# K and V of a head in three pieces (48, 32, 48 KB per partition) in place of four of 32 KB, in a ring lapped twice per head

## Chip, cores, metric

One core of a Trainium2 chip. The metric is the device time of one execution in microseconds (us), lower is better. The kernel has one stream of DMA transfers, issued by SyncE (its queue is "SPq" in the profile); TensorE (PE), VectorE (DVE) and ScalarE (ACT) work behind it.

## The reference, cut

One decode step of a transformer layer: layer norm, q projection, attention of 32 query heads over 8 K/V heads with 65536 keys each, output projection, residual, layer norm, gated feed-forward. K and V in bf16 are 16 MiB each per head, so nearly all of the 282 MB read is cache.

```python
q = (x @ wq).reshape(B, Sq, Hq, Dh) ...                 # Hq = 32, Hkv = 8, Dh = 128, Sk = 65536
scores = jnp.einsum("bhqd,bhkd->bhqk", q, k) * (Dh ** -0.5)
p = _softmax(scores, axis=-1)
o = jnp.einsum("bhqk,bhkd->bhqd", p, v)
return o...reshape(B, Sq, Hq * Dh) @ wo
# then h = x + that; h2 = h + (sigmoid(n(h) @ w_gate) * (n(h) @ w_up)) @ w_down
```

## The kernel before

A **chunk** is 4 KB per partition (16 keys of 128 elements). A block of K or V is 8 chunks, 32 KB per partition, 4 MiB in all; a head has four of each. The ring in SBUF has four such slots. The order of loads is K of a block, then V of the block one head earlier, and each load waits until the block that had its slot is done: a K block is done when DVE has transposed its chunks (mark `F`), a V block when PE has multiplied it (`PV`).

```python
order = [("wq", 0)]
order += [("K", b) for b in range(NR)]                      # NR = 4 blocks per head
for b in range(NR, NB):                                     # NB = 32 blocks in all
    order += [("K", b), ("V", b - NR)]
order += [("V", NB - 4), ("V", NB - 3), ("V", NB - 2), ("V", NB - 1), ("wg", 0), ("wu", 0), ("wd", 0)]
# ... slot_of[ld] = i % NSLOT, prev[ld] = order[i - NSLOT]   (NSLOT = 4; the last ones are placed by hand)

def freed(ld):
    ...
    return {"wq": "q", "K": f"F{b}", "V": f"PV{b}"}[k]
# ... each load: deps = [freed(prev[ld])]; wo (into the transposed K's space) waits for G7, the last maxima
```

DVE transposes each chunk into one of 8 work buffers, and after the eighth sets the mark, without waiting for anybody:

```python
def dve_block(b):
    s = slot_of[("K", b)]
    for c in range(NC):                                     # NC = 8 chunks
        ...
        op("dve", lambda e, d=dst, sr=src: e.transpose(d, sr), deps, f"T{b}.{c}", to="T")
    op("dve", lambda e: e.memset(scr[:, b:b + 1], 0.0), (), f"F{b}")
    # after a head's last block: maxima of the scores, then mark G
```

PE works per head in four parts: the scores of K block r of this head, then the products of V block r of the head before. Part 3 begins with the maxima of the scores and the softmax, so its products come last of all. A block's products are four rounds of 8 matmuls in a loop in registers; `p` and `v` are the addresses in the weights and in the ring.

```python
goto("sums", "values")
pv_regs(e)                                                  # 14 addresses from p and v
goto("products", "sums")
section("B")                                                # 8 matmuls
e.reg_alu(p, p, 2 * 512, ALU.add)
e.reg_alu(v, v, 2 * 2 * CH, ALU.add)
e.reg_alu(m, m, -1, ALU.add)
e.br_ne(m, 0, on_true="sums", on_false="sums_end")
```

Of the kernel before, what the change touches and what calls it, by code (L numbers as in the profile page):

```python
# [213 lines left out]
def bass_sequential_preLN__gqa_block_cached__glu_gated_glu__decode_kernel(  # L214
# [10 lines left out]
    SLOT = T * DH  # L225
    CH = TC * DH
    NF = FF // 128
# [6 lines left out]
    with ExitStack() as es:  # L234
# [16 lines left out]
        ring = sb("ring", [128, NSLOT * SLOT], bf16)  # L251
# [50 lines left out]
        def slot_ap(s):  # L302
            return ring[:, s * SLOT:(s + 1) * SLOT]

# [4 lines left out]
        order = [("wq", 0)]  # L309
        order += [("K", b) for b in range(NR)]  # L310
        for b in range(NR, NB):
            order += [("K", b), ("V", b - NR)]
        order += [("V", NB - 4), ("V", NB - 3), ("V", NB - 2), ("V", NB - 1), ("wg", 0), ("wu", 0), ("wd", 0)]
        slot_of, prev = {}, {}
        for i, ld in enumerate(order):
            if ld[0] == "V" and ld[1] >= NB - NR:
                slot_of[ld] = slot_of["V", ld[1] - 2]
                prev[ld] = ("V", ld[1] - 2)
            elif ld[0][0] == "w" and i:
                slot_of[ld] = 3 if ld[0] == "wd" else 1  # L320
                prev[ld] = ("K", NB - 1 if ld[0] == "wd" else NB - 2)
            else:
                slot_of[ld] = i % NSLOT
                prev[ld] = order[i - NSLOT] if i >= NSLOT else None

        def freed(ld):
            if ld is None:
                return None
            k, b = ld
            return {"wq": "q", "K": f"F{b}", "V": f"PV{b}"}[k]  # L330

        dma("act", lambda e: e.dma_start(x_col[:, :], A_x[0].rearrange("o (p k) -> (o p) k", k=4)), "x", name="x")
        V_SPLIT = [(0, 3), (3, 4)]
        W_SPLIT = {"wg": [(0, 4)], "wu": [(0, 3), (3, 4)]}
        W_AT = {"wg": 0, "wu": 4 * FF}
        for ld in order:
            k, b = ld
            s = slot_of[ld]
            dst = slot_ap(s)
            deps = [freed(prev[ld])]  # L340
            if k == "wq":
                dma("sp", lambda e, d=dst: e.dma_start(d.rearrange("p (k n) -> p k n", k=4),
                    A_wq.rearrange("(p k) n -> p k n", p=128)), f"r{s}", deps, "wq")
            elif k in ("wg", "wu"):
                w = B_w_gate if k == "wg" else B_w_up
                dst, src = dst[:, W_AT[k]:W_AT[k] + 4 * FF], w.rearrange("(p k) n -> p (k n)", p=128)
                for i, (k0, k1) in enumerate(W_SPLIT[k]):
                    dma("sp", lambda e, d=dst, w=src, a=k0 * FF, z=k1 * FF: e.dma_start(d[:, a:z], w[:, a:z]),
                        f"{k}{i}", deps if i == 0 else (), f"{k}.{i}")
            elif k == "wd":  # L350
                src = B_w_down.rearrange("(p r) n -> p r n", p=128)
                for i, (r0, r1) in enumerate(WD_SPLIT):
                    dma("sp", lambda e, d2=dst[:, r0 * D:r1 * D].rearrange("p (r n) -> p r n", n=D), sr=src[:, r0:r1, :]:
                        e.dma_start(d2, sr), f"wd{i}", deps if i == 0 else (), f"wd{i}")
            else:
                h, r = b // NR, b % NR
                cache = A_k_cache if k == "K" else A_v_cache
                src = cache[0, h, r * BLK:(r + 1) * BLK, :].rearrange("(p t) d -> p (t d)", t=T)
                if ld == ("V", NB - 1):
                    for i, (c0, c1) in enumerate(V_SPLIT):  # L360
                        d2, s2 = (ap[:, 2 * c0 * CH:2 * c1 * CH] for ap in (dst, src))
                        dma("sp", lambda e, d2=d2, s2=s2: e.dma_start(d2, s2),
                            "v0" if i else "vl", deps if i == 0 else (), f"V{b}.{i}")
                else:
                    dma("sp", lambda e, d=dst, sr=src: e.dma_start(d, sr), f"v{s}" if k == "V" else f"k{s}" if k == "K" and b >= NR else f"r{s}",
                        deps, f"{k}{b}")
            if ld == ("V", NB - 4):
                for i, (j0, nj) in enumerate(WO):
                    src = A_wo[j0 * DH:(j0 + nj) * DH, :].rearrange("(p r) n -> p (r n)", r=nj)
                    dst = ktw[:, j0 * D:(j0 + nj) * D]  # L370
                    dma("sp", lambda e, src=src, dst=dst: e.dma_start(dst, src), f"wo{i}",
                        [f"G{HKV - 1}"] if i == 0 else (), f"wo{i}")
# [81 lines left out]
        def project_q(e):  # L454

            e.reg_mov(reg(e, 0), addr_of(xz, 8 + 7))
            e.reg_mov(reg(e, 4), addr_of(ring, slot_of[("wq", 0)] * SLOT))
# [3 lines left out]
            with e.Fori(0, HKV):  # L461
                for kt in range(4):
                    mm_at(e, ps(1, 0, 512, 0, 8), at_reg(xz, reg(e, kt), [[4 * 16, 128], [1, 8]]),
                          at_reg(ring, reg(e, 4 + kt), [[NSLOT * SLOT, 128], [1, 512]]), False, 32)
                for kt in range(4):
                    e.reg_alu(reg(e, kt), reg(e, kt), 2, ALU.subtract)
                for kt in range(4):
                    e.reg_alu(reg(e, 4 + kt), reg(e, 4 + kt), 1024, ALU.add)
# [32 lines left out]
        def dve_block(b):  # L501
            s = slot_of[("K", b)]
            for c in range(NC):
                n = b * NC + c
                at = s * SLOT + (2 * (c % NR) + c // NR) * CH
                src = ring[:, at:at + CH].bitcast(fp32)
                dst = ktw[:, (n % NKT) * CH:(n % NKT + 1) * CH].bitcast(fp32)
                deps = [f"K{b}"] if c == 0 else []
                if b % NR or b == 0:
                    deps.append(f"S{b - 1}.{c}" if b else None)  # L510
                op("dve", lambda e, d=dst, sr=src: e.transpose(d, sr), deps, f"T{b}.{c}", to="T")  # L511
            op("dve", lambda e: e.memset(scr[:, b:b + 1], 0.0), (), f"F{b}")
# [62 lines left out]
        def pv_regs(e):  # L575
            for half in range(NC // NR):
                for tq in range(4):
                    i = 8 * half + tq
                    if i:
                        e.reg_alu(reg(e, i), R["p"], 2 * (128 * tq + half), ALU.add)  # L580
                        e.reg_alu(reg(e, i + 4), R["v"], 2 * (half * TC + 4 * tq) * 128, ALU.add)

        def pv(b):
            h, r = b // NR, b % NR
            if r == NR - 1:
                P.part["pe"] = ("VL", b)
                op("pe", lambda e: None, [f"V{b}" if b < NB - 1 else f"V{b}.1"])
            P.part["pe"] = ("B", b)
            for half in range(NC // NR):
                for tq in range(4):  # L590
                    i = half * 8 + tq
# [3 lines left out]
                        at_reg(ring, reg(e, i + 4) if i else R["v"], [[NSLOT * SLOT, 128], [1, 512]]), False, 32, 32 * tq),  # L595
                       (), f"PV{b}" if half and tq == 3 else None, times=NR)

        def head_out(h):
            op("act", lambda e: e.activation(po_sb[:, :], ps(PO, 0, 512), AF.Copy, scale=rl[:, :]),  # L599
               [f"PV{NR * h + NR - 1}", f"rl{h}"], f"po{h}", to="po")  # L600
# [68 lines left out]
        def pe_flow(e, section):  # L669
# [7 lines left out]
            i, w, p, v, m, k = (R.setdefault(n, e.alloc_register(f"r_{n}")) for n in "iwpvmk")  # L677
            w0, p0 = addr_of(ktw, W0 + NC - 1 + 127), addr_of(PT_sb, 31 * 4)
            v_even, v_odd = (addr_of(ring, slot_of[("V", b)] * SLOT) for b in (0, 1))
            e.reg_mov(i, 0)  # L680
            goto("head")
            e.reg_mov(w, w0)
            e.reg_mov(p, p0)
            goto("part")
# [13 lines left out]
            e.reg_mov(m, NR)  # L698
            e.reg_mov(k, 0)
            e.reg_mov(v, v_even)  # L700

            def odd_late():
                e.reg_mov(v, v_odd)
                e.reg_mov(m, NR - 1)
                e.reg_mov(k, 1)
                away("br_eq", i, HKV, "last_values", lambda: section("VZ"), "sums")
                section("V3")

            def odd():
                e.reg_mov(v, v_odd)  # L710
                section("V1")

            away("br_eq", w, w0, "values0", lambda: section("V0"), "sums")
            away("br_eq", w, w0 - 4, "values1", odd, "sums")
            away("br_eq", w, w0 - 12, "values3", odd_late, "sums")
# [5 lines left out]
            e.reg_alu(p, p, 2 * 512, ALU.add)  # L721
# [5 lines left out]
            def rest():  # L727
                pv_regs(e)
                e.reg_mov(m, 1)
# [7 lines left out]
            e.reg_alu(p, p, 4 - 2 * NR * 512, ALU.add)  # L737
# [7 lines left out]
            away("br_eq", w, w0 - 4, "rows_of_o", lambda: section("L"))  # L745
# [7 lines left out]
        def dve_flow(e, section):  # L753
            with e.Fori(1, HKV):
                for p in ("A0", "B0", "A1", "A2", "A3", "A4"):
# [4 lines left out]
                       "po": ("pe", {"V0": 1, "O": 1}), "v0": ("pe", {"V1": 16, "VL": 16}), "v2": ("pe", {"V0": 16, "V2": 16}),  # L760
                       "Q": ("dve", {"A4": NR * NC + 3}), "D": ("dve", {"A4": 6}), "E": ("dve", {"A4": 4}), "k1": ("dve", {"A4": 32}),
# [110 lines left out]
```

## Time and profile before

| | before |
|---|---|
| time, three runs | 658.1 us median (658.04 to 658.2) |
| span of the profiled run | 657.1 us |
| last landing of the DMA stream | 654.83 us |
| each of the 63 K and V loads of 4 MiB, landing to landing | 9.69 us, within 0.07 |

"Landing" is the moment at which the last of a transfer's 16 completions (one per DMA engine) is recorded in the trace.

In the median a block lands 26 to 29 us after its issue, because others are ahead of it. wq finds an empty queue at time zero and takes 12.3 us for what moves in 9.69: **2.6 us more**.

### The profile page before, as it was taken

How to read it: one execution, taken by the hardware profiler on the slowest of the kernel's cores; microseconds unless marked ns; L12 is line 12 of the kernel's file. 1: busy time of each engine (PE TensorE's matmuls, PEld its weight loads, DVE VectorE, ACT ScalarE, POOL GpSimd, SP SyncE). 2: the span in 40 equal slices, each digit the busy share in tenths (PEclk: the TensorE clock that was granted, in tenths of full speed). 3: DMA queues.
4: the chain of work that ended last, by engine and by line, in shares of the span. 5: the costliest groups of instructions: out<-in, count | busy, mean ns of one | idle time of the engine just before them, and what ended most of it. 6: DMA issues, size and time to landing. Idle time of an engine off the chain costs nothing. (4 is left out here: it accounts for less than half of the span.)

```text
span 657.1 us, 6111 instructions
## 1 busy us (share of the span) xinstructions
PE 420.5 (64%) x2315; PEld 74.1 (11%) x1547; DVE 349.7 (53%) x439; ACT 42.9 (7%) x114; POOL 3.6 (1%) x17
## 2 busy tenths in 40 slices
PE   0688488548666585576765575764866668556746
PEld 0200011011000010010100110101100001001322
DVE  2399775547537665347555374465743575542202
ACT  1100200020000200020000200002000100002001
POOL 1000000000000000000000000000000000000000
PEclk9989689677888697776966769765888869677676
DMA  9999999999999999999999999999999999999998
GB/s 383 447 433 429 439 423 431 431 447 415 447 415 447 437 425 447 415 447 419 443 441 421 447 415 447 423 439 443 419 447 415 447 427 435 445 417 427 435 430 352
DMA packets 10802, 282.34 MB, mean 430 GB/s; under 512 B 1329, under 2 KB 1330, under 8 KB 1842
## 3 DMA queue, kind: packets, MB, share of 16 engines
q1 hardware_dynamic: 10658, 282.33, 99.7%
q10 hardware_dynamic: 144, 0.00, 0.0%
HBM read 282.33 MB, written 0.00 MB: 430 GB/s over the span
## 5 line engine op out<-in xcount | busy, mean ns | idle before, releaser
L431 PE MATMUL PS<-ktw 128*128 128x512 bf16 x1024 | 299.9, 442 | 157.4 <-DVE ktw L511 153.6
L511 DVE STREAM_TRANSPOSE ktw<-ring 128x1024 f32<-128x1024 f32 x256 | 291.6, 1205 | 128.0 <-DMA ring<-in_A_k_cache_dram 128.0
L431 PE MATMUL PS<-ring,PT_sb 128*32 x1024 | 83.9, 455 | 23.6 <-issue 13.2
L431 PEld LDWEIGHTS PS<-ktw 128*128 x256 | 27.1, 106 | 408.2 <-issue 256.8
L565 DVE STREAM_TRANSPOSE PT_sb<-P_sb 128x512 bf16<-128x512 bf16 x32 | 20.2, 684 | 54.0 <-PE PS L602 52.3
L551 ACT ACTIVATE negmax<-PS 128x1 f32<-128x1 f32 x8 | 1.4, 171 | 520.6 <-PE PS L549 520.6
L431 PEld LDWEIGHTS PS<-ring,PT_sb 128*32 x1024 | 25.8, 116 | 79.8 <-issue 74.6
L516 DVE TENSOR_REDUCE M_sb<-PS 128x1 f32<-128x512 f32 x32 | 19.9, 684 | 25.5 <-PE PS L431 25.5
L555 ACT ACTIVATE P_sb<-PS,negmax 128x512 bf16<-128x512 f32 x32 | 21.6, 686 | 0.3
L572 DVE TENSOR_REDUCE lsum<-PS 128x1 f32<-128x4 f32 x8 | 1.3, 163 | 31.2 <-PE PS L570 31.2
L542 PE MATMUL PS<-identf,gm 128*1 128x128 f32 x16 | 3.4, 301 | 16.9 <-DVE gm L540 16.9
L616 DVE TENSOR_TENSOR Lw<-O,blk_of 128x896 bf16<-128x896 bf16 (+1 forms) x2 | 1.4, 683 | 20.6 <-ACT O L606 20.6
L402 PE MATMUL PS<-st,onesf 128*128 128x2 f32 x4 | 1.2, 362 | 16.1 <-DVE st L401 16.1
L431 PE MATMUL PS<-ring,xz 128*8 x32 | 9.2, 459 | 2.3 <-issue 2.3
L599 ACT ACTIVATE po_sb<-PS,rl 128x512 bf16<-128x512 f32 x8 | 5.5, 687 | 53.2 <-PE PS L431 53.2
L431 PE MATMUL PS<-ktw,O 128*1 x26 | 7.6, 464 | 0.0
L549 PE MATMUL PS<-one_f,gmrep 1*128 1x1 f32 x16 | 4.2, 330 | 5.0 <-DVE gmrep L546 5.0
L555 ACT ACTIVATION_READ_ACCUMULATOR P_sb<-PS,negmax 128x1 f32 x32 | 6.5, 202 | 0.0
L476 DVE STREAM_TRANSPOSE qt<-qh 32x512 bf16<-32x512 bf16 x1 | 0.7, 699 | 10.6 <-ACT qh L473 10.6
L602 PE MATMUL PS<-sel_bf,po_sb 128*128 128x4 bf16 x32 | 2.0, 168 | 6.4 <-ACT po_sb L599 6.4
L417 DVE CAST hT<-x_col 128x4 f32<-128x4 bf16 x1 | 0.2, 171 | 10.6 <-DMA x_col<-in_A_x_dram 10.6
L661 DVE COPY yr<-PS 1x512 f32<-1x512 f32 x1 | 0.7, 679 | 8.3 <-PE PS L659 8.3
(82 smaller groups left out, 74.0 us busy)
## 6 DMA issues: line engine op xcount, KB each, us to landing
ring<-in_A_k_cache_dram SPq DMA_DIRECT2D x32, 4096.0 KB, 28.7
ring<-in_A_v_cache_dram SPq DMA_DIRECT2D x31, 4096.0 KB, 26.4
ring<-in_A_wq_dram SPq DMA_DIRECT2D x1, 4096.0 KB, 12.3
ktw<-in_A_wo_dram SPq DMA_DIRECT2D x1, 3584.0 KB, 12.7
ring<-in_A_v_cache_dram SPq DMA_DIRECT2D x1, 3072.0 KB, 13.2
ring<-in_B_w_gate_dram SPq DMA_DIRECT2D x1, 1792.0 KB, 19.0
ring<-in_B_w_up_dram SPq DMA_DIRECT2D x1, 1344.0 KB, 21.7
ring<-in_A_v_cache_dram SPq DMA_DIRECT2D x1, 1024.0 KB, 15.2
```

The source lines that it names most:

```text
L431: return e.add_instruction(mybir.InstMatmult(name=nc.get_next_instruction_name(), engine=mybir.EngineType.PE, ins=[rhs, lhsT], outs=[e.low ...
L511: op("dve", lambda e, d=dst, sr=src: e.transpose(d, sr), deps, f"T{b}.{c}", to="T")
L516: op("dve", lambda e, u=u: e.tensor_reduce(M_sb[:, u % 4:u % 4 + 1], ps(u % NS, 0, 512), AX.X, ALU.max), [f"S{b}.{NC - NR + k}"], f"mx{u}" ...
L542: op("pe", lambda e: e.matmul(ps(MISC, 0, 128, 0, 1), lhsT=gm[:, :], rhs=identf[:, :], start=True, stop=True), [f"gm{h}"], f"gmT{h}", to="Q")
L549: op("pe", lambda e: e.matmul(ps(MISC, 128, 129), lhsT=gmrep[0:1, :], rhs=one_f[0:1, 0:1], start=True, stop=True), [f"gmrep{h}"], f"neg{h}")
L551: op("act", lambda e: e.activation(negmax[:, k:k + 1], ps(MISC, 128, 129), AF.Copy, scale=-att_scale), [f"neg{h}"], f"negmax{h}")
L555: op("act", lambda e, b=b: e.activation(P_sb[:, (b % 4) * 512:(b % 4 + 1) * 512], ps(b % NS, 0, 512), AF.Exp, bias=negmax[:, k:k + 1], sca ...
L565: op("dve", lambda e, b=b: e.transpose(PT_sb[:, (b % 4) * 512:(b % 4 + 1) * 512], P_sb[:, (b % 4) * 512:(b % 4 + 1) * 512]), [f"E{b}", f"o ...
L572: op("dve", lambda e: e.tensor_reduce(lsum[:, :], ps(MISC, 132, 136), AX.X, ALU.add), [f"l{h}"], f"ls{h}", to="D")
L599: op("act", lambda e: e.activation(po_sb[:, :], ps(PO, 0, 512), AF.Copy, scale=rl[:, :]), [f"PV{NR * h + NR - 1}", f"rl{h}"], f"po{h}", to ...
L602: op("pe", lambda e, t=t: e.matmul(ps(OX, 0, 4), lhsT=po_sb[:, t * 128:(t + 1) * 128], rhs=sel_bf[:, 8 * t:8 * t + 8:2], start=(t == 0), s ...
L616: op("dve", lambda e: e.tensor_tensor(Lw[i][:, :].rearrange("p (j c) -> p j c", j=n), bass.AP(tensor=O2, offset=j0, ap=[[NQ, 128], [1, n], ...
```

## The change

The intent is fewer and longer transfers: 48 pieces in place of 64 blocks. As 48 + 32 + 48 KB do not fit fixed slots, the ring's 32 chunks are laid out by hand: K.0 in chunks 0 to 11, V.0 in 12 to 23, K.1 in 24 to 31, V.1 in 0 to 7, K.2 in 8 to 19, V.2 in 20 to 31. A head thus laps the ring twice.

```diff
+    PIECES = ((0, 12), (12, 20), (20, 32))
+    RING = 32 * CH
+    AT = {"K": (0, 24, 8), "V": (12, 0, 20), "K0": (0, 12, 20), "wq": 24, "wg": 12, "wd": 8}
 ...  (loads: the old order, slot_of and freed are gone)
+        for h in range(1, HKV + 1):
+            old = h - 2
+            before_k = (["F0.1"], ["G0"], [f"F{h}.1"]) if h == 1 else ([f"PV{old}.2"], [f"PV{old}.3"], [f"F{h}.1"])
+            before_v = (["F0.3"] if h == 1 else [f"PV{old}.3"], [f"F{h}.0"], [f"F{h}.2"])
+            if h < HKV:
+                for q in range(3):
+                    load("K", h, q, before_k[q], ("ka", "kb", "ka")[q], f"K{h}.{q}")
+                    load("V", h - 1, q, before_v[q], ("va", "vb", "va")[q], f"V{h - 1}.{q}")
+                continue
+            load("V", h - 1, 0, before_v[0], "va", f"V{h - 1}.0")
+            for i, (j0, nj) in enumerate(WO):
 ...              (wo, waits for G7)
+            load("V", h - 1, 1, (), "vb", f"V{h - 1}.1")
 ...              (V.2 in two parts behind PV7.1, then w_gate, w_up, w_down)
 ...  (DVE: the marks that free K's space)
-            op("dve", lambda e: e.memset(scr[:, b:b + 1], 0.0), (), f"F{b}")
+                mark = {7: 0, 11: 1, 19: 2}.get(j, 3 if b == 2 and c == 7 else None)
+                if mark is not None:
+                    op("dve", lambda e, m=4 * h + mark: e.memset(scr[:, m:m + 1], 0.0),
+                       [f"S{b}.{c}"] if mark in (1, 2) else (), f"F{h}.{mark}")
 ...  (PE: the products of a head in parts of 4, 2, 4 and 6 rounds)
+        PARTS = (4, 2, 4, 6)
+            step = (2 * 2 * 512, 2 - 2 * 2 * 512)
             section("B")
-            e.reg_alu(p, p, 2 * 512, ALU.add)
+            e.reg_alu(p, p, s, ALU.add)
+            e.reg_alu(s, s, step[0] ^ step[1], ALU.bitwise_xor)
             e.reg_alu(v, v, 2 * 2 * CH, ALU.add)
```

The mark after chunk j of a head waits for that chunk's scores (`S`) when it is mark 1 or 2. `PV{h}.r` is the end of part r of the products.

## The prediction

> **What bounds the kernel now.** I read the page first, for what is full:
>
> ```profile
> span 657.1 us, 6111 instructions
> PE 420.5 (64%) x2315; PEld 74.1 (11%) x1547; DVE 349.7 (53%) x439; ACT 42.9 (7%) x114; POOL 3.6 (1%) x17
> ...
> DMA  9999999999999999999999999999999999999998
> ...
> PE 1%; DVE 0%; issue 0%; ACT 0%
> ```
>
> The DMA engines are full from the first slice to the last; no compute engine is above 64%; the chain that ended last holds about 1% of the span in compute. So the kernel is one uninterrupted stream of 282.34 MB, plus about 1 us before its first byte (in the windows, 0 GB/s up to 1.0 us) and about 2.5 us after its last (bytes stop between 654 and 655 us). The windows view over two heads' worth of quiet middle gives the rate:
>
> ```profile
> 254.60:293.40 38.80, 23.38 (x112) 3.35 (x68) 21.40 (x26) 2.63 (x8) 0.00 (x0) 0.72 1.00 432
> ```
>
> 432 GB/s, so a 4 MiB block (32 KB per partition) takes 9.70 us, which the timeline repeats: two K starts two blocks apart are at 254.63 and 274.03.
>
> Then the waits of the DMA queue, because a stream can only stay full if the next transfer is issued in time:
>
> ```profile
> SPq L365 <- DVE scr L512: 324.2, 30, 19.4
> SPq L365 <- PE PS L431: 222.4, 29, 18.8
> ```
>
> The issuing queue waits nearly all the time, for a K slot to be transposed (DVE) or a V slot to be multiplied (PE). None of this costs anything today: a transfer lands 26 to 29 us (median) after its issue while it moves for 9.7 us, so over one and a half blocks are queued ahead. That reserve is what the change alters. Last I read the timeline at the end of the last head, the chain from a K landing to the release of V's space:
>
> ```profile
> 583.83 9.13 DVE L511 STREAM_TRANSPOSE ktw<-ring 128x1024 f32<-128x1024 f32 x8 [10.27 <-DMA ring<-in_A_k_cache_dram]
> ...
> 588.51 8.49 PE L431 MATMUL PS<-ktw 128*128 128x512 bf16 x29 [0.54 <-DVE ktw L511]
> ...
> 596.39 2.48 DVE L516 TENSOR_REDUCE M_sb<-PS 128x1 f32<-128x512 f32 x4 [3.42 <-PE PS L431]
> ...
> 598.92 0.80 SPq L371 DMA_DIRECT2D ktw<-in_A_wo_dram  x2
> ...
> 602.45 2.76 PE L431 MATMUL PS<-ring,PT_sb 128*32 x24 [1.75 <-issue]
> ...
> 605.50 1.02 PE L431 MATMUL PS<-ring,PT_sb 128*32 x8 [0.29 <-PEq L169]
> 606.57 8.66 SPq L365 DMA_DIRECT2D ring<-in_A_v_cache_dram  x2
> ```
>
> A head's last K lands at 583.8, is transposed by 592.9, scored by 597.0, its maxima taken, and the last quarter of the previous head's products ends at 606.5; the next V is issued at 606.57. That is 22.7 us from landing to release. The same interval at the other heads (K block landing to the V issue after the head's last products) is 21.4 to 23.4 us. Before the change it is hidden: another V block and then wo are already queued behind.
>
> **What the Trainium skill says.** "DMA: Bandwidth & Descriptors", section "Where 436 GB/s comes from": the ceiling of the 16 ports is 435.2 GB/s. The trace runs at 432, so at most 0.7% is left. Same page, "Why small descriptors are slow": a fixed overhead of about 3 cycles per packet, plus descriptor metadata. The trace agrees in size: 9.70 us per block against 9.64 at 435.2 GB/s. Same page, "Anatomy of one DMA": the DMA engines wait on no semaphore; the issuing sequencer does, before dispatch. The queue's waits above show just that, so one late release holds back everything behind it. "Perfetto Trace Analysis", "DMA Optimizations": larger transfers saturate HBM better, but its example is under 2 KB; at 32 KB this trace has nothing such to gain.
>
> **The change part by part.**
>
> (1) Fewer, longer transfers: 64 blocks of K and V become 48 pieces, and the runs per partition 48, 32 and 48 KB. The whole overhead of the 64 blocks is 64 x (9.70 - 9.64) = about 4 us; a quarter of it goes: **-1 us**. Bytes are the same. A 48 KB piece is an estimated 14.55 us, a 32 KB one 9.70.
>
> (2) The steady head. The ring is still 128 KB, now 32 chunks of 4 KB. Order and places: K.0 in chunks 0-11, V.0 12-23, K.1 24-31, V.1 0-7, K.2 8-19, V.2 20-31. The next head's V.0 overlaps V.2 and waits for part 3 of the products, which reads all of V.2 and comes after all scores and the maxima; the next K.0 waits for part 2. Take the landing of K.2 as zero. V.2 lands at 14.55; K.0 of the next head, if on time, ends at 28.8 (29.1 less 0.3 from last byte to signal). Part 2: four transposes of 1.14 (4.6), the rest of that block's scores (about 13 matmuls of 0.27, to 8.2), four rounds of products (2.2 warm): release near 10.5, first byte 1.0 to 1.2 later, ahead of 14.3. On time, by 2 to 3 us. Part 3: the 22.7 us chain of before (mean of the heads 22.5), plus four more transposes since the piece has 12 chunks (4 x 1.14 = 4.6), plus about 1.5 since PE must do that half block and part 2 first and starts the last scores later, plus two more rounds of products (six for four, 0.6 to 0.7 each after the saved extra wait: 1.3). Release at about 29.9, first byte at 31.1, but the queue is empty at 28.8. **About 2.4 us of idle DMA per head; with PE at its lower clock up to 4.5, with everything warm about 1.** It happens for the V.0 of heads 1 to 6: six times, **+15 us**.
>
> (3) The last head. There is no next K.0 to cover V.0 of head 7, and wo stands behind that V.0 in the queue. So when V.2 of head 6 has landed nothing is queued. The last byte is at 14.3, release at 29.9, first byte at 31.1: **+17 us** in one piece. Before, V and wo filled this hole.
>
> (4) The start. The marks that free K space now wait for scores (after chunks 11 and 19), and DVE stands at them. In the first head DVE is the pace (its row in the timeline is unbroken from 29.0 to 65.2, 1.13 per transpose), so each mark costs the 16 matmuls it waits for, 3.8 us plus hand-over: about 7.8 for both. The head's end mark moves from 70.1 to 78. In before, the next K block's mark came 14.8 later (84.96), so the release for V.1 of head 0 comes near 92.8, first byte at 94; the stream would be empty when K.1 of head 1 is in, which by bytes is 9 blocks and wq from the start, about 89.6. That is 4.4 late. The K.2 behind it waits for scores that are late as well: 1 to 2 more. **+6 us.** If x, on its own small queue, arrives a packet later, add 1.
>
> (5) The end. The last V piece is 32 and 16 KB for 24 and 8; two rounds after the final landing for one (0.8 us), but PE no longer lags behind as it did, and the weights behind are as many bytes as before. **About 0.** The extra register instruction per round is inside the 0.76 us round.
>
> Sum: 658.1 - 1 + 15 + 17 + 6 + 0.5 = **about 696 us**, 5.7% slower.
>
> **The rivals.** (A) *The pieces only remove overhead*: all releases come in time, 657 us. For it: the DMA row is full, compute stands at two thirds. Against it: the average says nothing about a release that is serial after a landing; at least the hole in (3) follows from program order alone. It would need V.0 of head 7 to be released before V.2 of head 6 has landed, which cannot be. (B) *Only the ends lose*: PE is in better clock with longer bursts (the windows show 0.5 to 0.6 of full clock around the maxima), the steady release comes 2 to 3 us earlier, and (2) vanishes: 658 - 1 + 16 + 5 = 678. Speaks for it: the margin is only 2.4 us out of 30. Against: the chain is mostly fixed waits, and part 3 always begins after a pause of PE. (C) *The steady wait is larger*: PE falls to its lower clock for the whole of part 3 (0.92 a round, six rounds) and the late scores (0.3 a matmul), 4.5 to 5 us a head, and the start costs 9: 658 - 1 + 29 + 18 + 9 = 713. (D) *48 KB runs move slower*, from another row pitch in HBM or a split of the runs. Nothing in the trace speaks for it: runs of 32, 28 and 24 KB go at one rate. One per cent of rate would be 6.5 us.
>
> **Range and chances.** The certain part is (3), 15 to 19. (2) spans 6 to 29, (4) 3 to 9. The ends of all together are 681 and 715; 8 in 10 is 682 to 712. The 2% line is 671.3: to stay under it (2) and (4) must both nearly vanish. Slower 0.94, within 2% 0.05, faster 0.01.
>
> **What would show it.** In the profile after: a DMA row with a single low slice near 93 to 95% of the span, some 17 us in which the windows show no bytes, ended by a V issue released by PE; six shorter holes of 2 to 3 us, about 80 us apart, each just before the V.0 that follows a K.0; holes totalling 5 to 8 us between 85 and 110 us; mean near 406 GB/s; the rate between holes 432 to 433, which checks (1). The reading is wrong if the DMA row stays at nines, or if the idle time is there but in front of K.0 (then part 2 is the late release), or if the rate between holes is lower (rival D).

## More of the kernel before

The page's list of DMA issues (last column: median us from issue to landing) shows both:

```profile
ring<-in_A_k_cache_dram SPq DMA_DIRECT2D x32, 4096.0 KB, 28.7
ring<-in_A_v_cache_dram SPq DMA_DIRECT2D x31, 4096.0 KB, 26.4
ring<-in_A_wq_dram SPq DMA_DIRECT2D x1, 4096.0 KB, 12.3
```

The **lead** of a transfer is the landing of the transfer ahead of it minus its own issue: how much time the queue still had in hand when it was issued. Its **loss** is landing, minus the landing ahead, minus its bytes at 9.69 us per 4 MiB. In the kernel before the smallest lead is 4.2 us and only the very first transfer, wq, loses anything.

## The result

| | before | after |
|---|---|---|
| time, six runs each, side by side | 658.24 us (658.04 to 658.39) | 719.02 us (716.85 to 720.74) |
| ratio | | 1.0922 (95%: 1.0904 to 1.0940) |
| span of the profiled run | 657.1 us | 715.5 us |
| last landing | 654.83 us | 713.33 us |

A ratio here is the mean time of one kernel's fast runs over that of the other's fast runs of the same rounds, so not quite the ratio of the medians quoted. The output is correct. The time was predicted as 696 us with a range up to 712: the direction was right, the size 23 us short. The kernel before spent 2.3 us after its last landing, the kernel after 2.2, so the whole 58 us of the two profiled runs lie in the stream.

From the page of the kernel after, first the counts and rows by slice (40 slices of 17.9 us; "DMA" in tenths busy), then the chain that ended last, then one group of instructions, then two kinds of DMA issue:

```profile
span 715.5 us, 6263 instructions
...
DMA  9999989979999799979999899988999899926998
GB/s 410 419 431 393 426 310 396 423 324 427 438 440 426 327 432 438 426 313 433 434 434 393 346 415 450 429 371 355 432 434 420 332 430 437 429 129 280 423 430 348
...
DMA 7%; PE 2%; issue 1%; SPq 0%; DVE 0%; PEldq 0%
...
L498 DVE MEMSET scr<- 1x1 f32 x25 | 1.5, 59 | 66.0 <-PE PS L414 66.0
...
ring<-in_A_k_cache_dram SPq DMA_DIRECT2D x16, 6144.0 KB, 20.4
ring<-in_A_v_cache_dram SPq DMA_DIRECT2D x15, 6144.0 KB, 17.6
```

The nines have dips: one about every 4.6 slices, which is once per head, and one of 2 at the end (129 GB/s). DVE stands 66 us at its marks. The last row is the plainest: half of the 48 KB V pieces land within 17.6 us of their issue, for a transfer that moves in 14.5. They find a dry or nearly dry queue, as wq did.

One head of the kernel after, from the timeline (start, length, engine, line, what, count, in brackets the idle time before it and its releaser):

```profile
287.62 13.64 DVE L495 STREAM_TRANSPOSE ktw<-ring 128x1024 f32<-128x1024 f32 x12 [9.86 <-DMA ring<-in_A_k_cache_dram]
...
298.44 0.63 PE L414 MATMUL PS<-ring,PT_sb 128*32 x8 [0.39 <-issue]
...
299.12 0.33 SPq L322 DMA_DIRECT2D ring<-in_A_k_cache_dram  x1
...
300.08 7.10 PE L414 MATMUL PS<-ktw 128*128 128x512 bf16 x32 [1.00 <-issue]
...
306.56 2.49 DVE L503 TENSOR_REDUCE M_sb<-PS 128x1 f32<-128x512 f32 x4 [5.31 <-PE PS L414]
...
312.60 6.05 PE L414 MATMUL PS<-ring,PT_sb 128*32 x48 [1.93 <-PEq L169]
...
318.69 0.33 SPq L322 DMA_DIRECT2D ring<-in_A_v_cache_dram  x1
```

K.2 lands at 287.59. Part 2 of the products ends at 299.1 and the next K.0 is issued; V.2 lands at 302.09, K.0 at 317.63. Only after the last scores, the maxima and six rounds of products is V.0 issued, at 318.69: 31.1 us after K.2 landed and 1.06 us after the queue ran dry. It lands at 336.30, 17.6 us later. The windows view of the kernel after around that point and before the last head's V.0 (window, length, busy time and count of PE, PEld, DVE, ACT, POOL, granted clock, DMA share, GB/s; a packet is counted in the window in which it starts):

```profile
315.00:317.30 2.30, 2.30 (x24) 0.32 (x16) 0.00 (x0) 0.00 (x0) 0.00 (x0) 0.50 0.06 21
317.40:319.60 2.20, 1.41 (x16) 0.32 (x12) 0.00 (x0) 0.69 (x1) 0.00 (x0) 0.69 0.00 0
632.40:650.00 17.60, 11.42 (x82) 2.07 (x62) 3.14 (x8) 3.65 (x10) 0.00 (x0) 0.90 0.00 0
```

In the first window one packet starts, on one engine of 16 (0.06); in the second none. In the third, 17.6 us long, none either: the hole that the prediction's third term is about. No such window exists in the kernel before.

**The accounts.** Landing by landing, the kernel after loses:

| where | losses (lead in brackets) | sum | predicted |
|---|---|---|---|
| start: V0.0, V0.1, K1.2 | 2.80 (0.45), 3.64 (-1.19), 2.99 (-0.09) | 9.4 | 6 |
| K.0 of heads 2 to 7 | 1.0 to 2.55 (1.6 to 3.0) | 11.2 | 0 |
| V.0 of heads 1 to 6 | 2.3 to 4.1 (-1.06 to 0.32) | 18.9 | 15 |
| V.0 of head 7 | 19.34 (-16.45) | 19.3 | 17 |
| the 14 pieces of 48 KB with over 5 us of lead | -0.036 each | -0.5 | -1 |

Sum 58.5 before rounding; the last landing is 58.5 us later. No other transfer loses more than 0.1, but for wq with 2.6 in both kernels, which is not in the sum. The pieces as such do what they were to do: a 6 MiB piece in an uninterrupted stream lands every 14.50 us, against 14.535 for one and a half old blocks. Everything lost is lost at transfers that were **issued late**.

The two steady rows are one effect, not two. The queue is back at one point in each head: V.0. From K.2's landing to the next one, a head lasts

31.1 (release of V.0) + 17.4 (V.0, issue to landing) + 9.69 (K.1) + 9.69 (V.1) + 14.54 (K.2) = **82.4 us**,

and the mean of the six steady heads is 82.46, against 77.5 without losses. So a loss of K.0 costs nothing of its own as long as V.0's release comes behind it. The prediction's numbers in the same sum: 29.9 + 16.05 + 33.9 = 79.9. It missed 1.2 in the release and 1.4 in V.0's issue to landing, six times: 15 of the 23 us. Its third term missed the same 1.2 and 1.4 once more (19.3 for 17), its fourth 3.4; the rest is that the median run is 2.2 us slower than the profiled one, which was the fastest of six.

**Why an issue 0 to 4 us ahead still costs.** The trace has the 16 completions of each transfer (the 1st, 8th, 15th and 16th in order of completion, us), here for one steady block of the kernel before and four consecutive pieces after; the first line of each is a reference:

```
before  K block       254.34  254.47  254.57  254.61
        next V block  264.02  264.17  264.30  264.35
after   V.2           300.93  301.27  302.03  302.09
        K.0, lead  3.0  315.50  315.86  316.52  317.63     nominal: V.2 + 14.54
        V.0, lead -1.1  335.00  335.48  336.12  336.30
        K.1, lead 17.2  344.68  345.15  345.76  345.95     V.0 + 9.69
```

K.0's first 15 engines are on time to within 0.1 us; **one engine is 1.0 us late, and the transfer has landed only when it has**. At other heads it is two or more of them (head 5: 399.49, 399.77, 401.36, 401.76). In the kernel before the 16 completions of a load lie within 0.25 to 0.44 us of each other; after a late issue they lie 0.7 to 2.4 us apart, and the pieces behind it keep the spread (1.27 to 1.34 us in the four behind the V.0 above). The packet records show where this begins: V.0's first packets start 0.95 us after its issue, and take 2.0 to 3.5 us (mean of the 16: 2.6) where nearly all later ones take 1.82. 0.95, the slowest engine's 1.7, and the usual few tenths from last byte to landing make about the 2.9 us that a dry queue costs a 48 KB piece on average. What makes the first packets slow, the traces do not tell.

The same records account for the uneven loss at small positive leads. K.0 above starts on each engine within 0.01 us of V.2's end there, yet its first packets take 1.81 to 2.52 us, and the one of 2.52 is the last to start. In this run and in experiments 4 and 6 together, 28 transfers have leads of 0.6 to 5 us; in 24 of them the latest end of a first packet is late by the loss itself, to within 0.4 us. (The records do not name the engine; packets were matched to transfers by their order in time.) So the loss depends on where a slow first packet falls: one K.0 of experiment 6 (issued at 442.86, lead 3.5) has first packets of up to 2.81 us and loses 0.03, as they fall on engines with time in hand.

### The profile page after: what moved, and what is told of

It reads as the page before. It is cut to its first block, busy times and chain, and to the rows that moved or that the text cites. A ratio compares the mean times of both kernels' runs of the same rounds, so it can differ in the third digit from the quotient of the medians.

```text
span 715.5 us, 6263 instructions
## 1 busy us (share of the span) xinstructions
PE 426.9 (60%) x2315; PEld 67.7 (9%) x1547; DVE 350.6 (49%) x432; ACT 43.0 (6%) x114; POOL 3.6 (1%) x17
## 5 line engine op out<-in xcount | busy, mean ns | idle before, releaser
L414 PE MATMUL PS<-ktw 128*128 128x512 bf16 x1024 | 294.7, 438 | 173.8 <-DVE ktw L495 159.1
L414 PE MATMUL PS<-ring,PT_sb 128*32 x1024 | 94.6, 474 | 58.0 <-PEq L169 40.0
L414 PEld LDWEIGHTS PS<-ring,PT_sb 128*32 x1024 | 21.2, 116 | 133.3 <-issue 130.4
L498 DVE MEMSET scr<- 1x1 f32 x25 | 1.5, 59 | 66.0 <-PE PS L414 66.0
## 6 DMA issues: line engine op xcount, KB each, us to landing
ring<-in_A_v_cache_dram SPq DMA_DIRECT2D x15, 6144.0 KB, 17.6
ring<-in_A_wq_dram SPq DMA_DIRECT2D x1, 4096.0 KB, 12.3
```

Of the source, the lines that this page charges most:

```text
L414: return e.add_instruction(mybir.InstMatmult(name=nc.get_next_instruction_name(), engine=mybir.EngineType.PE, ins=[rhs, lhsT], outs=[e.low ...
L498: op("dve", lambda e, m=4 * h + mark: e.memset(scr[:, m:m + 1], 0.0), [f"S{b}.{c}"] if mark in (1, 2) else (), f"F{h}.{mark}")
```

## The experiments

The theory: (T1) all of the loss is late issue; the release of V.0 sets each head's period, V.0 of head 7 the end, DVE's waiting marks the start; and a late issue costs more than its lateness. The rivals: (T2) 48 KB runs or the ring's new layout are slower in themselves; (T3) only lateness beyond the queue's end costs, and the rest is something else, such as the added register instructions per round. All kernels below are correct, and each was timed against the kernel before of the same rounds (658.2 to 658.8 us).

### 1. wo ahead of the last head's V.0

```diff
-            load("V", h - 1, 0, before_v[0], "va", f"V{h - 1}.0")
             for i, (j0, nj) in enumerate(WO):
                 ...
+            load("V", h - 1, 0, before_v[0], "va", f"V{h - 1}.0")
```

> The changed kernel, but with wo issued ahead of V.0 of the last head instead of behind it. Theory A (the loss is a late release, and an issue that finds the queue empty costs about 2.9 us plus the time it is late): wo waits for the last head's maxima, which in the changed kernel ended 21.4 us after K.2 landed; V.2 lands 14.5 after it. So wo loses 6.9 + 2.9 = 9.8 us, V.0 then finds wo still moving (issued about 3 us before wo has landed) and loses 0 to 2. Together 10 to 12 us where the changed kernel lost 19.3: 710 to 712 us. Rival B (the hole at the end is not on the path that sets the end, because PE has to finish the last products anyway): no gain, 719.

Measured: **719.6 us** (716.57 to 721.03), ratio 1.0907. The hole became smaller: wo loses 11.0 at a lead of -8.4, V7.0 1.6, and V7.2, now without wo ahead of it, 2.9, together 15.5 in place of 19.3. The time did not follow. The page's chain and the timeline of this run:

```profile
PE 5%; DMA 3%; issue 1%; DVE 1%; ACT 0%; PEldq 0%
```

```profile
643.73 0.80 SPq L340 DMA_DIRECT2D ktw<-in_A_wo_dram  x2
...
652.86 29.32 SPq L322 DMA_DIRECT2D ring<-in_A_v_cache_dram  x4
...
683.15 8.29 PE L414 MATMUL PS<-ktw,O 128*1 x26
...
705.23 1.60 PE L414 MATMUL PS<-ring,PT_sb 128*32 x16 [0.51 <-issue]
```

V7.0 now lands at 672.2, 5.6 us later than in the kernel after (2.7 of these were lost before the last head, whose K.2 lands at 620.8 for 618.2; 3.0 come from the new order), and behind it lies serial work of PE: two parts of products, the rows of the output projection (683 to 691), two more parts. The chain is PE's, and the span ends 7.6 us after the last landing in place of 2.2. Theory A's 710 to 712 missed that, and the number came out as the expectation's rival B had it, but not its reason: in the kernel after the hole was on the path that sets the end (2.2 us from the last landing to the end). Once it was shortened, the gain was **given back on another path**. What follows: the last head's hole is a matter of order, but which transfer fills it has to be chosen with PE's tail in view.

### 2. Marks that do not wait in the first head

```diff
-                       [f"S{b}.{c}"] if mark in (1, 2) else (), f"F{h}.{mark}")
+                       [f"S{b}.{c}"] if h and mark in (1, 2) else (), f"F{h}.{mark}")
```

> The changed kernel, but in the first head the marks after chunks 11 and 19 no longer wait for scores (there are no V reads to protect yet, so this is free of races). Theory A: DVE stands 3.1 and 3.7 us less, the releases of V.0 and V.1 of head 0 and K.2 of head 1 come about 7 us earlier, and the 9.4 us that these three pieces lost (2.8, 3.6 and 3.0) shrink to 0 to 3: 710 to 713 us. Rival B (PE sets the pace of the first head, the marks only stand where DVE would have waited anyway): 718 to 719.

Measured: **714.84 us** (714.68 to 715.87), ratio 1.0855, about 4.2 us less than the kernel after. First the kernel after, then this one, DVE and the first V issue from the timelines:

```profile
47.59 1.24 DVE L495 STREAM_TRANSPOSE ktw<-ring 128x1024 f32<-128x1024 f32 x1 [3.08 <-issue]
...
60.44 1.24 DVE L495 STREAM_TRANSPOSE ktw<-ring 128x1024 f32<-128x1024 f32 x1 [3.72 <-issue]
...
65.11 0.33 SPq L322 DMA_DIRECT2D ring<-in_A_v_cache_dram  x1
```

```profile
45.12 9.12 DVE L495 STREAM_TRANSPOSE ktw<-ring 128x1024 f32<-128x1024 f32 x8
...
57.68 0.33 SPq L322 DMA_DIRECT2D ring<-in_A_v_cache_dram  x1
```

DVE's two pauses of 3.1 and 3.7 us are gone and the releases come 7 to 8 us earlier. The losses at the start fall from 9.4 to 3.3 us, and head 1's K.2 lands 6.0 earlier; about 4 of those are lost again further on (six periods of 82.88 for 82.46, last hole 20.7 for 19.3), so that the two profiled spans differ by 2.0 only. Losses of that size lie within the kernel's own spread (its repeat in experiment 7 has a period of 82.66 and a hole of 20.6). So the marks are the cause of the start's loss.

### 3. A ring of 36 chunks, so that V.0 need not wait for V.2

```diff
-    RING = 32 * CH
+    RING = 36 * CH
-    AT = {"K": (0, 24, 8), "V": (12, 0, 20), ...
+    AT = {"K": (0, 24, 8), "V": (12, 0, 24), ...
-            before_v = (["F0.3"] if h == 1 else [f"PV{old}.3"], ...
+            before_v = (["F0.3"] if h == 1 else [f"G{h - 1}"], ...
```

V.2 moves to chunks 24 to 35 and no longer overlaps V.0, which then waits for the maxima (`G`) alone; V.2 gets a semaphore of its own.

> The changed kernel on a ring of 36 chunks instead of 32: V.2 lies in chunks 24 to 35, no longer over the place of the next V.0, which then waits for the end of its head's maxima (21.4 us after K.2 lands) instead of for the last products (31 us). Pieces, their sizes and K.0's release stay. Theory A: the six V.0 that lost 18.9 us together lose nothing; the hole at the end shrinks from 19.3 to 21.4 - 14.5 + 2.9 = 9.8; K.0 keeps its loss of 1 to 2.5 a head (11 us): 719 - 18.9 - 9.5 = 690 to 692 us. Rival B (48 KB runs are slow by themselves): the loss stays near the pieces of 48 KB, at most the hole at the end changes: 708 or more.

Measured: **687.88 us** (687.18 to 691.59), ratio 1.046, 31 us less than the kernel after. From the page, and from the timeline one head's two issues:

```profile
DMA  9999988999999999999999999999999999958998
```

```profile
294.74 0.33 SPq L322 DMA_DIRECT2D ring<-in_A_k_cache_dram  x1
...
304.73 0.33 SPq L322 DMA_DIRECT2D ring<-in_A_v_cache_dram  x1
```

V.0 is issued 10 us behind K.0 (19.6 in the kernel after), with a lead of 7.4 to 9.6 us, and loses nothing in heads 1 to 6. The dips between the start and the end are gone. K.0's lead is still 1.6 to 2.4 from head 3 on, and it still loses 1.0 to 1.8, which now counts: the period is 78.96. The end hole is 10.5 us. The same 48 KB runs in nearly the same ring lose half as much, which speaks against T2, and shows that V.0's release sets the period.

### 4. The kernel before, with late issues and nothing else

13 K blocks of the kernel before wait for a later mark of DVE, placed so that the lead becomes 0.2 to 6.2 us. Runs, slots and the products' loop are as they were.

```diff
             deps = [freed(prev[ld])]
+            if k == "K" and b in LATE:
+                lb, lc = LATE[b]
+                deps = [f"F{lb}" if lc == 7 else f"M{lb}.{lc}"]      # M: a mark behind the transpose of that chunk
```

> The kernel before with its 32 KB pieces, but 13 of its K blocks (two at each head boundary) are issued late on purpose, at a mark after transpose 2 to 7 of the block two ahead in the queue, so that they are issued 6.2, 5.0, 3.9, 2.8, 1.6 and 0.5 us before the block ahead of them has landed. It measures what a late issue costs, with pieces of 32 KB. Theory A (an issue less than about 3 us before the queue runs dry costs 2 to 3 us, whatever the size): the seven with 2.8, 1.6 and 0.5 lose 2 to 2.9 each, the six others nothing: 14 to 20 us, 672 to 678 us. Rival B (a late issue costs only what is left of 1.1 us to the first byte, and the rest is the price of 48 KB runs): only the two with 0.5 lose, 0.6 each: 659 to 660 us.

Measured: **672.11 us** (670.75 to 673.29), ratio 1.020 (1.0179 to 1.0222). No issue came after the queue's end, and the time is 13.7 us longer all the same; 11.7 of these are in the stream (last landing 666.54), the rest lies outside the profiled span. Loss by lead: 0.23: 2.28; 0.40: 2.04; 1.38: 1.73; 1.57: 0.96; 2.58: 1.36 and 1.25; 2.87: 0.47; 3.73: 0.56; the five late blocks from 4.1 up: 0. (These losses sum to 10.7; the other 1 us is 0.1 to 0.3 at a few V blocks behind them, at leads of 13 to 18.) This refutes T3 on the queue: **to be safe, a transfer has to be issued about 4 us before the queue runs dry**, by more than its 0.95 us to the first byte. It is a margin and not a sharp edge: in the kernel after three transfers with leads of 2.9 to 3.8 lost nothing, and in the other runs up to 0.7 us was lost at leads of 4.1 to 4.5. It is also the picture of the 16 completions again: behind the issue at a lead of 2.58, the 1st and 15th engine complete at 278.68 and 279.37, the 16th at 280.76, and the following six loads keep a spread of 1.8 to 2.1 us, where the kernel before has 0.3.

### 5. Two rounds of products per pass of the loop

The chunk that a round reads alternates between two strides, for which the change has one more register instruction in the source and a stride that is held in a register. In the trace a round then has three register instructions before its branch (starts 313.65, 313.75, 313.85, branch at 313.95), where the kernel before has a single one (214.30, branch at 214.41) for the same counters. Here a pass does two rounds, each with its own addresses, and neither the alternating stride nor the exclusive-or is needed. Half of the branches go as well.

```diff
             section("B")
-            e.reg_alu(p, p, s, ALU.add)
-            e.reg_alu(s, s, step[0] ^ step[1], ALU.bitwise_xor)
-            e.reg_alu(v, v, 2 * 2 * CH, ALU.add)
+            pv_regs(e, 2)
+            section("C")
+            e.reg_alu(p, p, 2, ALU.add)
+            e.reg_alu(v, v, 4 * 2 * CH, ALU.add)
```

> The changed kernel, but its loop of products does two rounds per pass, so the register that alternates the step (two more register instructions a round) is gone. In the changed kernel a round takes 0.97 to 1.02 us where it took 0.76 before. If those two instructions are the reason (theory A), rounds go back to about 0.76, part 3 releases the next V.0 1.2 us earlier (30 instead of 31.2 us after K.2 lands) and part 2 releases K.0 0.8 us earlier, at about 3 to 3.7 us ahead of the landing before it instead of 2.2 to 3. K.0 then loses 0 to 0.6 instead of 1 to 2.5, V.0 about 3 as before since its queue also ends sooner, the hole at the end shrinks by 1.2: 719 less about 13, 704 to 709 us. Rival B (the rounds are slow because PE is at its lower clock, the registers are hidden): rounds stay at 0.97 and the time within 2 us of 719.

Measured: **712.91 us** (711.02 to 714.62), ratio 1.0829, 6 us less than the kernel after and about half of what was hoped for. The weight loads in the timelines show a round's beat (each row is one round's eight loads), first before, then after, and then the six rounds of part 3 in this experiment (6.05 us in the kernel after, above):

```profile
214.27 0.16 PEld L431 LDWEIGHTS PS<-ring,PT_sb 128*32 x8 [2.04 <-issue]
...
215.04 0.24 PEld L431 LDWEIGHTS PS<-ring,PT_sb 128*32 x8 [0.61 <-issue]
```

```profile
313.62 0.16 PEld L414 LDWEIGHTS PS<-ring,PT_sb 128*32 x8 [0.86 <-issue]
...
314.59 0.16 PEld L414 LDWEIGHTS PS<-ring,PT_sb 128*32 x8 [0.81 <-issue]
```

```profile
310.54 4.71 PE L414 MATMUL PS<-ring,PT_sb 128*32 x48 [1.73 <-PEq L169]
```

0.77 to 0.83 us a round before and 0.97 to 1.02 after; here the six rounds take 4.71 us in place of 6.05, 0.22 us a round less, at nearly the same granted clock (0.58 from 310.6 to 315.2, and 0.56 in the kernel after from 311.0 to 318.6). By the starts above, **0.2 us a round** is what the two extra instructions take; this experiment alone does not separate them from the branch that went with them. Ten rounds lie in front of V.0's release. That release moves from 31.1 to 29.0 us behind K.2's landing, as it should. But V.0's issue to landing grows from 17.4 to 18.8, since it is now issued with a lead of 1 to 1.85 us, behind a K.0 that is itself landing late, and still loses 1.9 to 3.6. The period falls by 0.8 only. In this range of leads an earlier issue earns less than half of itself.

### 6. All remedies together

Ring of 36, free marks in the first head, two rounds per pass, and at the end V7.1 before V7.0, then wo, then V7.2 without waiting for part 1.

> All causes taken away at once, with the 48, 32 and 48 KB pieces kept: ring of 36 chunks, no waiting marks in the first head, two rounds per pass, and at the end V.1 of the last head first (released by part 2), then V.0 (released by the maxima), then wo, then V.2. Theory A (late issues are the whole loss, the pieces themselves cost nothing): start 0 to 3, K.0 0 to 0.6 in six heads, the end 0 to 2: 659 to 665 us. Rival B (pieces of 48 KB cost by themselves): the loss stays above 10 us, 668 or more.

Measured: **670.57 us** (667.1 to 671.89), ratio 1.0168. No hole is left; the remaining losses are at K1.2 (2.5, lead 0.45), V0.2 (1.6, lead 2.45), at four of the six K.0 (0.6 to 2.1, leads 2.9 to 3.3) and at the tail (0.5, 0.6, 0.5). That is nearly all in the band of partial leads again. By its number alone this run falls to rival B (668 or more), not to theory A's 659 to 665; the landings show that no undisturbed 48 KB piece is slow, and experiment 8 tests it.

### 7. Run length: 16 KB runs in three kernels, and the kernel after once more

If long runs make a restart dear, then the same transfers cut into 16 KB runs should pay less. Three kernels: the one of experiment 4, the kernel before, and the kernel after, each with 16 KB runs per partition for the K and V transfers, all transfers and releases as they were. Beside them the kernel after, unchanged.

```diff
-            rows = cache[0, h, j0 * TC * 128:j1 * TC * 128, :].rearrange("(p t) d -> p (t d)", p=128)
+            rows = cache[0, h, a * TC * 128:z * TC * 128, :].rearrange("(n p t) d -> p n (t d)", p=128, n=(z - a) // 4)
```

> The kernel before with the same 13 late K blocks as the earlier experiment, but every K and V block (except the last) is read as two runs of 16 KB per partition instead of one of 32 KB, keys of K and V permuted alike. Question: does the price of a late issue depend on the length of the runs? If it does (theory A2: the first run on each engine after a dry queue is slow in proportion to its length), the late blocks lose about half of the 10.6 us they lost: 5 to 6 us over the same kernel with 16 KB runs and no late block. If it does not (rival B2: the price belongs to the transfer, not to its runs), 10 to 12 us over it.

> The kernel before with 16 KB runs and nothing late: the steady price of shorter runs, and the zero for the run with late blocks. Twice as many runs; the whole overhead of the 32 KB runs was about 4 us over the kernel, so 3 to 4 us more if it goes by run (661 to 662), 658 if it goes by transfer.

> The changed kernel, its pieces, places, releases and waits kept, but every piece read as two or three runs of 16 KB instead of one of 48 or 32 KB. Theory A2 (the price of a late issue goes with the length of the runs): the late K.0, V.0 and the start lose a third to a half of their 2 to 3 us, 15 late pieces times about 1 us, less 3 to 4 us for more runs: 706 to 712. Rival B2 (the price is of the transfer): 719 plus 3 to 4.

> The changed kernel unchanged, on the same chip as the three others, for comparison: 717 to 721 us; its releases follow the same chain, so the late pieces are again every V.0 and K.0, each within 1.5 us of the first profile.

Measured: late issues with 16 KB runs **675.69 us** (674.53 to 677.26); before with 16 KB runs **660.74** (660.5 to 662.52); after with 16 KB runs **711.22** (710.99 to 712.1); after again **720.51** (718.54 to 721.16).

The steady price of short runs is 2 us (0.033 us per load in the trace). The price of the late issues is then 675.7 - 660.7 = 15 us with 16 KB and 672.1 - 658.4 = 13.7 with 32 KB, or by the last landings 11.6 (668.96 - 657.39) and 11.7: no smaller with short runs. In the changed kernel, though, short runs save 9.3 us: V.0's issue to landing is 16.75 in place of 17.48, the period 82.04 for 82.66, K.2 of head 1 lands 3.4 earlier, the last release comes 1.1 earlier. At leads up to 0.6 us the cost of the dry queue, loss plus lead, is 2.2 us for the 6 MiB pieces with 16 KB runs and 2.9 with 48 KB. For 4 MiB loads it is 2.3 to 2.55 with 16 KB runs and as much, 2.4 to 2.5, with 32 KB (experiment 4, and V.1 of head 0 in the kernel after). So run length is part of the price of a *dry* queue for the long pieces, and only a small part; for the 4 MiB loads, and at small positive leads, it does not show. Why they differ stays open.

The repeat also shows the kernel's own spread. Its profiled run, 3.4 us longer in span than the first one, has its releases later: 31.3 for 31.1 on average, 32.1 for 30.9 at the end, and head 1's K.2 0.7 later.

### 8. Part 2 of the products earlier as well

Experiment 6 and one thing more: PE does part 2 of the products right behind part 1, before the scores of K.2; K.0 then waits for part 2 and for a mark of DVE.

```diff
-            before_k = ... ([f"PV{old}.2"], ...
+            before_k = ... ([f"PV{old}.2", f"F{h - 1}.3"], ...
```

> The combined kernel of before (36 chunks, no waiting marks in the first head, two rounds per pass, other order at the end), and in addition the products of part 2 are done right after part 1, as soon as V.1 has landed, so that the next K.0 waits only for the first four transposes of K.2 (about 4.7 us after its landing, 9.8 us ahead of V.2's landing). Pieces of 48, 32 and 48 KB stay. Theory A (late issues are the whole loss): K.0 loses nothing in any head; what is left is K.2 of head 1 (2.5 us) and V.2 of head 0 (1.6) at the start and about 1 us at the end; the longer runs give back 1 us: 660 to 664 us. Rival B (48 KB pieces cost by themselves beside the late issues): 667 or more, as the combined kernel.

Measured: **666.79 us** (664.75 to 670.2), ratio 1.0139. From the page:

```profile
span 664.4 us, 5951 instructions
...
DMA  9999998999999999999999999999999999999996
```

K.0 is released 4.9 us behind K.2's landing, and every piece of the steady heads has a lead of 5.2 us or more. None of them loses anything: 29 unhurried 48 KB pieces at -0.036 each. What is left is the start (K1.2 2.1 at a lead of 0.8, V0.2 4.1 at -0.9), 0.4 at the tail, and 3.9 us from the last landing to the end for 2.3. The time is above theory A's 660 to 664 and just under rival B's 667, so it decides nothing; the landings do. This closes T2: with the same three pieces and the same runs, in time, the stream is as full as before. No version here beats the kernel before; at best the pieces save 31 times 0.036, about 1 us.

## Why the prediction was wrong in size

- **"-1 us" for fewer, longer transfers: right as a price.** 0.036 us per 48 KB piece in an undisturbed stream, about 1 us for all 31; here only 14 came in time and earned 0.5.
- **The mechanism of the steady head: right.** V.0 waits for part 3 of the products, which the ring's double lap puts behind the maxima, and the queue has run dry by then. Experiment 3 shows it.
- **"Release at about 29.9": 1.2 us short.** The step that failed is in part (5): "The extra register instruction per round is inside the 0.76 us round." A round went to 0.97 to 1.02 us. In the trace two instructions are added, and the weight loads of before already showed that rounds come at PE's issue pace ("idle before: issue"), so an added instruction there adds time: about 2.0 us in ten rounds, which other terms of the sum, 0.8 too long, hid in part. Experiment 5 agrees.
- **"First byte at 31.1, but the queue is empty at 28.8 ... about 2.4 us": the step that failed most.** The prediction priced an empty queue at its time to the first byte. That time was right, 0.95 us measured for the 1.0 to 1.2 taken; but the first packets take 2.6 us on average for 1.82, up to 3.5, and the landing waits for the slowest of 16 engines: 2.9 us in all. The wq line of the page of before, 12.3 us for a 9.7 us transfer, carried that number, and it was not read.
- **K.0 "on time, by 2 to 3 us": not on time.** Its release was put at 10.5 and came at 11.95, the four slow rounds of part 2 among the causes. But 1.6 to 3.0 us of lead were left, and it lost 1.0 to 2.6 all the same; experiment 4 shows that this is what such a lead costs. Here it cost nothing of its own, as V.0 set the period. Where V.0 is in time (experiments 3 and 6), it is the loss. One of the prediction's own signs of a wrong reading, time lost "in front of K.0", thus came true in part, beside the loss expected at V.0.
- **"+17" for the last head: right in kind, 19.3 in size**, by the same two terms.
- **"+6" for the start: right in kind, 9.4 in size.** The marks do cost DVE two pauses, 6.8 us with hand-over where 7.8 were taken, and experiment 2 shows them as the cause. Three transfers then came with leads of 0.45, -1.19 and -0.09, and each lost 2.5 to 3.3 us less its lead. The prediction had the last two of them late; the first, V.0 of head 0, which cost 2.8, it did not name. (Its "9 blocks and wq" should read nine blocks' worth with wq among them; its 89.6 is right for that.)
- **The rivals.** (C), "the steady wait is larger", named 713 us and comes nearest, but by luck: its reason was PE's lower clock, and experiment 5's rounds are shorter at nearly the same clock. (D), slower 48 KB runs, is refuted for the steady stream by the 14.50 us and by experiment 8; a longer restart with longer runs, which was on no list, has a small part (experiment 7). (A) and (B) did not happen. Of the signs listed, the single low slice came at 88 to 90% of the span, not at 93 to 95%.

**Open:** what makes the first packet on each engine slow after a late issue; what decides which engines get a slow one; and why run length shows for the 6 MiB pieces at a dry queue, but not for 4 MiB loads or at small leads.

## What to carry to other kernels

A stream that is full is full because of its reserve, so price a new layout by the lead it leaves each transfer, not by its number of transfers. On this stream a transfer that was issued under 4 us before the queue ran dry already cost up to 2.3 us (experiment 4; up to 3.6 behind pieces that were late themselves, experiment 5), and an issue into a dry queue on average 2.2 to 2.9 on top of the lateness; here the first transfer of the kernel before, with its 2.6, had shown that price. Before changing the order at an end, follow both paths: what fills the queue's hole may push back what another engine does serially (experiment 1).

## What the Trainium skill lacked or had wrong

- **"DMA: Bandwidth & Descriptors", section "Latency and other measured facts"**, gives about 600 ns to the first byte for a queue driven by SyncE. Here the first packets start 0.95 to 1.03 us after an issue into an empty queue, and the full price there, issue to landing less the bytes, is 2.2 us (6 MiB in 16 KB runs), about 2.45 (4 MiB in 32 KB runs) and 2.9 (6 MiB in 48 KB runs).
- **"SBUF — State Buffer", section "The DMA setup-cost knee"**, has every transfer pay a roughly fixed 2 us that does not scale with bytes, mostly for completion, and advises the largest single transfer. That is near the price of a transfer alone. In a queue with another transfer ahead it was zero here (14.50 us landing to landing for 6 MiB, 9.69 for 4 MiB), so merging transfers had only about 1 us to win.
- None of the pages read says **how far ahead of a draining queue a transfer has to be issued**. Here it was about 4 us: 0.5 to 2.3 us lost at leads of 0.2 to 3.7 us, none by the late blocks from 4.1 up in experiment 4. Nor that the completions of the 16 engines spread at a late issue (0.25 to 0.44 us before, 0.7 to 2.4 after) and that the spread stays for the transfers behind.
- None of them gives the price of **a register instruction in a loop of small matmuls**: two more per round of eight, 0.1 us each by their starts, took a round from 0.77 to 0.83 us to 0.97 to 1.02.
